# Gate logits of three of four chunks moved from TensorE to DVE, gate rows loaded earlier, key masks shared between DVE and POOL

## Chip, cores, metric

One core of a Trainium2 chip. The metric is device time in microseconds (us); lower is better. PE is TensorE, ACT is ScalarE, POOL is GpSimd, SP the queue that issues most DMAs, and PEld the weight loads, which run beside PE's matmuls.

## The reference, cut to what matters

A gate per token mixes an attention block with memory (four segments of 512 tokens, which the kernel calls chunks) and a gated feed-forward block.

```python
g = sigmoid((x * gate_w).sum(-1, keepdims=True))      # one logit per token: 2048 x 512 times 512
a = attention_with_memory(x, wq, wk, wv, wo, beta)     # 32 heads of 16, segments of 512, memory carried over
b = (relu(x @ W_gate) * (x @ W_up)) @ W_down           # 512 -> 1792 -> 512
return g * a + (1 - g) * b
```

## The kernel before: what the argument touches

The program describes every operation with its possible engines, an estimated duration, and the names that it reads and writes. A list scheduler in Python then walks through modelled time, puts each operation on an engine, and writes down one fixed instruction list per engine with semaphore waits. So any change of a duration or of an operation changes the order on all engines. Engines run their lists in order: a wait at the head of a list holds up everything behind it.

The loads, in order of issue (most on SP, two `wq` tiles on ACT):

```python
# hT0..3 (rows of x, chunk 0), wq, wk, wv, then:
load("sp", ["braw"], V.braw[:], A_beta.partition_broadcast(128), 8192)
load_gu(0)                                             # first halves of W_gate and W_up, 8 x 224 KB
load("sp", ["g4"], V.g4[:], gate_w.rearrange("(kt p) -> kt p", p=128), 1 << 12)   # the gate rows, 1 KB
load_gu(1)                                             # second halves
load_x(1)                                              # chunk 1 of x, 4 DMA transposes -> xT
load("sp", ["wo"], ...)
load("sp", ["wd"], V.wd[:], ..., NF * 128 * 1024)      # 1.8 MB, in one DMA
```

The gate logits: one small matmul turns the gate rows into columns (`gwT`), then one-column matmuls on PE, 16 for chunk 0 and 48 for chunks 1 to 3.

```python
gw_pe = pe(... matmul(A(ep_w)[:, 0:KT], lhsT=V.g4, rhs=V.ident[0:KT, 0:KT]) ..., name="gwT")
for part, (t0, t1) in enumerate(((0, 4), (4, NT))):
    def f_gmm(e, ...):
        for t in range(t0, t1):
            for kt in range(KT):
                ins = e.matmul(A(ep_g)[:, t - t0:t - t0 + 1], lhsT=V.xT[:, kt, t*128:(t+1)*128], rhs=V.gwc[:, kt:kt+1], ...)
```

Keys: `kT` is evicted, masked twice by DVE for the attention (`kmask`), and, for the memory, its exp goes into `ek`, is adjusted by DVE and transposed by a DMA into `phik`. `ek` has one buffer per head group, so the exp of the next chunk must wait until that transpose has read it.

```python
for p in range(2):
    evs.append(dve(... tensor_scalar(V.kp[:, ks, :], V.kT[:, G, :], V.pm[:, p:p+1], None, ALU.mult), 417, ...))   # kmask
acts.append(act(... activation(V.ek[:, G, :], V.kT[:, G, :], ACT.Exp) ..., writes=[f"ek{G}"]))
sps.append(dma("sp", ... dma_start_transpose(V.phik[:, :, G*128:(G+1)*128], V.ek[:, G, :]), reads=[f"ek{G}"], ...))
```

The softmax here doesn't subtract the row's maximum and nothing guards it: scores larger than these inputs give would overflow.

## Time and profile before

| | before |
|---|---|
| time, median of 6 runs | 276.43 us (275.97 to 276.89) |
| span of the profiled run | 274.8 us |
| first matmul, last matmul start | 1.25 us, 271.53 us |
| PE hole ahead of `gwT` | 0.82 us |
| 48 gate matmuls of chunks 1 to 3 | 1.2 us |

The busy line of the page of before, then the first two lines of its chain of waits (shares of the span, by engine and by line):

```profile
PE 269.2 (98%) x2205; PEld 116.2 (42%) x2205; DVE 200.1 (73%) x391; ACT 191.2 (70%) x167; POOL 91.4 (33%) x152
...
PE 91%; SPq 3%; DVE 2%; DMA 2%; issue 0%; ACT 0%
PE psA L731 37%; PE psA L770 18%; PE psL L661 9%; PE psA L686 7%; PE psA L566 7%; PE psA L564 5%; PE psA L763 5%; SPq L413 3%; DMA g<-in_gate_w_dram 2%; PE psA L607 1%; PE psA L636 1%; PE psA L522 1%; DVE ttmp L585 1%; DVE ek L586 0%; DVE rdm L629 0%
```

The chain is PE, but for one DMA: the 1 KB of gate rows. Here is that place in the timeline of PE (start, duration, engine, line, operation, count, idle time just before and what ended it):

```profile
13.72 0.40 PE L661 MATMUL psL<-qT,kp 32*128 32x512 bf16 x4
14.04 1.04 PE L564 MATMUL psA<-wv,xT 128*128 128x512 bf16 x4
15.73 0.17 PE L512 MATMUL psA<-ident,g 4*128 4x4 bf16 x1 [0.65 <-DMA g<-in_gate_w_dram]
```

Matmuls of 512 columns start every 0.216 us, and the printed ends are modelled. Four of them from 14.04 us are done streaming at 14.90 us, so PE stands still for 0.82 us, though the page prints 0.65. The gate matmuls of chunks 1 to 3:

```profile
54.59 1.34 PE L522 MATMUL psA<-gwc,xT 128*128 128x1 bf16 x48
55.87 0.40 PE L661 MATMUL psL<-qT,kp 32*128 32x384 bf16 x8
```

They take 25 ns each: 48 times 25 ns is 1.2 us for almost no arithmetic. The Trainium skill, "TensorE: Matmul & The Clock Gate", section "Wait — 56ns, not 53.3ns?", states this floor of about 25 ns between the starts of tiny matmuls, and the trace agrees (25.1 ns between the 48 starts). A third place that matters later are small holes where PE waits for DVE:

```profile
83.90 1.03 PE L566 MATMUL psA<-xT,wq 128*128 128x512 bf16 x4
84.98 1.04 PE L566 MATMUL psA<-xT,wk 128*128 128x512 bf16 x4
85.95 0.40 PE L661 MATMUL psL<-qT,kp 32*128 32x384 bf16 x8
86.51 2.33 PE L564 MATMUL psA<-wv,xT 128*128 128x512 bf16 x10 [0.17 <-DVE kT L579]
```

From 83.90 us four matmuls should end at 84.77; the next starts 0.21 us later. At 85.95 stand attention quads (a quad is four score matmuls of 32 rows that start within 0.01 us); the next matmul usually comes 0.33 us on; here 0.56. With one of 0.11 us at 117 us these holes make 0.55 us.

### The profile page before, as it was taken

The page shows a single profiled execution, that of the slowest core. Times are in us where ns is not written, and L with a number is a line of the kernel's source. Part 1 is how long each engine was busy: PE and PEld are TensorE (multiplying, and loading weights), DVE is VectorE, ACT ScalarE, POOL GpSimd, SP SyncE. Part 2 cuts the span into 40 slices and gives each one's busy share as a digit, 9 for nine tenths or more (in the row PEclk, how much of TensorE's full clock was granted, in tenths as well). Part 3 has the DMA queues.
Part 4 walks back from the last instruction along what each step waited for, and adds up shares of the span by engine and source line. Part 5 has one row for each costly group of instructions (what it writes and reads, how often), then busy time and mean ns, then how long its engine had stood idle before and what let it go on. Part 6 is the DMA issues. An engine that isn't in the chain of part 4 may idle for free.

```text
span 274.8 us, 5394 instructions
## 1 busy us (share of the span) xinstructions
PE 269.2 (98%) x2205; PEld 116.2 (42%) x2205; DVE 200.1 (73%) x391; ACT 191.2 (70%) x167; POOL 91.4 (33%) x152
## 2 busy tenths in 40 slices
PE   7999999999999999999999999999999999999995
PEld 3433434444343544534434444434444343444444
DVE  5779989999989969999789855396874256787200
ACT  3279898887787687778579777875867768773012
POOL 4013244353234434534243333243233343330000
PEclk9999999999999999999999999999999999999999
DMA  6999752100011122020012000100011100000011
GB/s 228 288 360 259 189 93 61 21 2 20 2 20 38 41 60 57 21 57 2 0 38 41 1 21 22 38 0 2 20 38 21 38 21 19 2 1 2 0 38 38
DMA packets 29152, 15.30 MB, mean 56 GB/s; under 512 B 20552, under 2 KB 29128, under 8 KB 29128
## 3 DMA queue, kind: packets, MB, share of 16 engines
q1 hardware_dynamic: 28552, 14.43, 20.6%
q10 hardware_dynamic: 576, 0.52, 0.6%
q8 instruction: 17, 0.28, 0.4%
q14 instruction: 7, 0.06, 0.1%
HBM read 8.14 MB, written 2.10 MB: 37 GB/s over the span
## 4 chain that ended last, share of the span: by engine, by line
PE 91%; SPq 3%; DVE 2%; DMA 2%; issue 0%; ACT 0%
PE psA L731 37%; PE psA L770 18%; PE psL L661 9%; PE psA L686 7%; PE psA L566 7%; PE psA L564 5%; PE psA L763 5%; SPq L413 3%; DMA g<-in_gate_w_dram 2%; PE psA L607 1%; PE psA L636 1%; PE psA L522 1%; DVE ttmp L585 1%; DVE ek L586 0%; DVE rdm L629 0%
## 5 line engine op out<-in xcount | busy, mean ns | idle before, releaser
L666 ACT ACTIVATE E<-psL 128x2048 bf16<-128x2048 f32 x80 | 150.1, 1876 | 41.3 <-PE psL L661 40.9
L669 POOL TENSOR_SCALAR_AFFINE_SELECT E<-E 128x512 bf16<-128x512 bf16 x128 | 81.3, 653 | 149.1 <-ACT E L666 134.0
L731 PE MATMUL psA<-xT,wu 128*128 128x512 bf16 x224 | 59.9, 380 | 0.0
L731 PE MATMUL psA<-xT,wg 128*128 128x512 bf16 x224 | 59.7, 380 | 0.0
L770 PE MATMUL psA<-wd,hT 128*128 128x512 bf16 (+1 forms) x238 | 54.3, 367 | 0.0
L742 DVE TENSOR_TENSOR hT<-psA,rl 128x512 bf16<-128x512 f32 x56 | 38.3, 684 | 12.6 <-PE psA L731 11.3
L661 PE MATMUL psL<-qT,kp 32*128 32x384 bf16 (+3 forms) x512 | 31.7, 301 | 0.0
L770 PEld LDWEIGHTS psA<-wd,hT 128*128 128x128 bf16 x238 | 21.8, 98 | 23.2 <-issue 3.0
L731 PEld LDWEIGHTS psA<-xT,wu 128*128 128x128 bf16 x224 | 20.6, 98 | 25.6 <-issue 2.0
L691 DVE STREAM_TRANSPOSE Tn<-psA 128x512 f32<-128x512 f32 x32 | 21.5, 700 | 13.0 <-PE psA L686 12.9
L731 PEld LDWEIGHTS psA<-xT,wg 128*128 128x128 bf16 x224 | 19.6, 98 | 24.6 <-issue 5.0
L739 ACT ACTIVATE rl<-psA 128x512 bf16<-128x512 f32 x30 | 17.8, 596 | 14.1 <-PE psA L731 14.1
L661 PEld LDWEIGHTS psL<-qT,kp 32*128 32x128 bf16 x512 | 8.9, 92 | 31.9 <-ACT E L666 14.4
L686 PE MATMUL psA<-E,vaug 128*17 128x256 bf16 (+3 forms) x512 | 21.0, 300 | 0.0
L740 DVE TENSOR_SCALAR rl<-psA 128x512 bf16<-128x512 f32 x26 | 17.8, 684 | 3.2 <-PE psA L731 2.5
L566 PE MATMUL psA<-xT,wq 128*128 128x512 bf16 x64 | 16.1, 380 | 0.3 <-DMA wq<-in_A_wq_dram 0.2
L763 PE MATMUL psA<-wo,oT 128*128 128x512 bf16 (+1 forms) x68 | 16.4, 367 | 0.0
L566 PE MATMUL psA<-xT,wk 128*128 128x512 bf16 x64 | 16.3, 380 | 0.1
L780 ACT ACTIVATE osb<-psA,omg 128x512 bf16<-128x512 f32 (+1 forms) x10 | 6.4, 644 | 14.1 <-PE psA L763 13.3
L564 PE MATMUL psA<-wv,xT 128*128 128x512 bf16 x64 | 15.5, 380 | 0.2 <-DVE kT L579 0.2
L686 PEld LDWEIGHTS psA<-E,vaug 128*17 128x17 bf16 x512 | 10.5, 90 | 11.0 <-issue 2.1
L779 DVE TENSOR_SCALAR osb<-psA,omg 128x512 bf16<-128x512 f32 x7 | 5.2, 745 | 12.6 <-PE psA L770 12.6
(71 smaller groups left out, 218.3 us busy)
## 6 DMA issues: line engine op xcount, KB each, us to landing
out_dram<-osb SPq DMA_DIRECT2D x15, 128.0 KB, 1.7
wg<-in_B_W_gate_dram SPq DMA_DIRECT2D x8, 224.0 KB, 4.9
wu<-in_B_W_up_dram SPq DMA_DIRECT2D x8, 224.0 KB, 5.5
wd<-in_B_W_down_dram SPq DMA_DIRECT2D x1, 1792.0 KB, 9.6
wk<-in_A_wk_dram SPq DMA_DIRECT2D x4, 128.0 KB, 4.4
wv<-in_A_wv_dram SPq DMA_DIRECT2D x4, 128.0 KB, 3.9
wo<-in_A_wo_dram SPq DMA_DIRECT2D x1, 512.0 KB, 5.1
hT<-in_A_x_dram SPq DMA_DIRECT2D x2, 128.0 KB, 2.7
```

The source lines that it names most:

```text
L564: ins = e.matmul(A(ep)[:, :], lhsT=V.xT[:, kt, tok + col * 128:tok + (col + 1) * 128], rhs=w[:, kt, :], start=(kt == 0), stop=(kt == KT - 1))
L566: ins = e.matmul(A(ep)[:, :], lhsT=w[:, kt, col * 128:(col + 1) * 128], rhs=V.xT[:, kt, tok:tok + 512], start=(kt == 0), stop=(kt == KT - 1))
L661: ins = q.matmul(PL[:, jj, o:o + w], lhsT=V.kp[32 * jj:32 * jj + 32, kslot(s, n), 128 * j:128 * j + 128], rhs=V.qT[32 * jj:32 * jj + 32, q ...
L666: acts.append(act(lambda a, e=e: a.activation(V.E[:, e, :, :], PL[:, :, :], ACT.Exp, scale=SCALE), t_act(2048), reads=[f"bankL{b}" for b i ...
L669: pools.append(pool(lambda g, ap=ap: g.affine_select(out=ap, in_=ap, compare_op=ALU.is_ge, fill=0.0, base=0, pattern=[[0, 4], [1, 128]], c ...
L686: ins = q.matmul(A(ep)[32 * jj:32 * jj + 17, c:512], lhsT=V.vaug[:, s % 2, j, 8 * G + 2 * jj + p, :], rhs=V.E[:, e, jj, o:o + w], start=(j ...
L691: ds.append(dve(lambda e, p=p, ep=eps[p]: e.transpose(V.Tn[:, p, :], A(ep)[:, :]), t_dve(512), writes=[f"Tn{p}"], name=f"tr{s}_{G}_{p}", e ...
L731: ins = e.matmul(A(ep)[:, :], lhsT=w[:, kt, f * 128:(f + 1) * 128], rhs=V.xT[:, kt, c * 512:(c + 1) * 512], start=(kt == 0), stop=(kt == K ...
L739: evs.append(sc.add(Op([("act", lambda e, ep=eg, r=r: e.activation(V.rl[:, r, :], A(ep)[:, :], ACT.Relu), t_act(512)), ("dve", lambda e, e ...
L742: evs.append(dve(lambda e, ep=eu, r=r, hs=hs: e.tensor_tensor(V.hT[:, hs, :], A(ep)[:, :], V.rl[:, r, :], ALU.mult), t_dve(512), reads=[f" ...
L763: ins = e.matmul(A(ep)[:, 0:c1 - c0], lhsT=V.oT[:, o0 + G, i * 128:(i + 1) * 128], rhs=V.wo[:, G, c0:c1], start=st_ and G == 0, stop=sp_ a ...
L770: ins = e.matmul(A(ep)[:, 0:c1 - c0], lhsT=V.hT[:, slots[f], i * 128:(i + 1) * 128], rhs=V.wd[:, f, c0:c1], start=st_ and f == f0, stop=sp ...
```

## The change

Its intent is to shorten PE's list (DVE computes 12 of the 16 tiles' logits), to end the wait for the gate rows, and to relieve DVE of key masks where POOL is free. Cut to its core:

```diff
 # loads
+    load("act", ["g4"], V.g4[:], gate_w..., 1 << 12)          # right behind wq on the ACT queue
     load_gu(0)
-    load("sp", ["g4"], V.g4[:], gate_w..., 1 << 12)
     load_gu(1)
     load_x(1)
+    load("sp", ["gwb"], V.gwb[:], gate_w.partition_broadcast(128), 1 << 17)
 # gate logits: chunk 0 on PE as before; chunks 1 to 3:
+            for t in range(t0, t1):
+                ld = dma("sp", ... dma_start(V.osb[:, 2, :], A_x[0, t*128:(t+1)*128, :]) ..., name=f"ldxr{t}")
+                ld.after = GATE_T[c] + 4000.0 * (t - t0)      # 44, 90, 140 us
+                gq["dve"].append(dve(... tensor_tensor_reduce(out=V.osb[:, 2, :], in0=V.osb[:, 2, :], in1=V.gwb[:], op0=ALU.mult, op1=ALU.add, accum_out=V.gl[:, t:t+1]) ...))
+            gq["act"].append(act(... activation(gx, V.gl[:, t0:t1], ACT.Exp) ...))
 # ... omg, gexpT copies and c2g per chunk instead of in two parts (64 small copies instead of 32)
 # key masks of chunks 1 to 3
-                evs.append(dve(... tensor_scalar(V.kp..., V.kT..., V.pm[:, p:p+1], None, ALU.mult), 417, ...))
+                alts = [("dve", km, 390)] + ([("pool", km, 680)] if s else [])
+                evs.append(sc.add(Op(alts, ...)))
 # output staging of chunks 0 to 2 uses two buffers of three; modelled time of the denominator matmuls halved
```

The full diff also reads `gexpT`, `c2g` and `omg` by chunk; nothing else depends on it.

More of the change, by code (lines that the diff above doesn't have):

```diff
@@ L16 @@
 SWITCH = 100.0
+GATE_T = {1: 44000.0, 2: 90000.0, 3: 140000.0}
 def mm(n, k=1):
@@ L353, in plan @@
         ("gwc", [128, KT], BF16), ("braw", [128, 32], BF16), ("eb", [128, 32], F32), ("romgh", [128, 32], F32), ("epsv", [128, 32], F32),
-        ("gexp", [128, NT], F32), ("omg", [128, NT], F32), ("gexpT", [128, NT * 4], F32), ("c2g", [128, NT, 32], F32),
+        ("gexp", [128, NT], F32), ("omg", [128, NT], F32), ("gexpT", [128, NT * 4], F32), ("c2g", [128, 2, 4, 32], F32), ("gwb", [128, 512], BF16), ("gl", [128, NT], F32),
         ("rden", [128, 32], F32), ("rdg", [128, 32], F32), ("rdm", [128, 128], F32), ("pm8", [128, 8], F32), ("pm", [128, 2], F32), ("ident", [128, 128], BF16), ("g4", [4, 128], BF16),
@@ L419, in program @@
             load("act" if nm == "wq" and kt % 2 else "sp", [f"{nm}{kt}"], w[:, kt, :], src[kt * 128:(kt + 1) * 128, :], 1 << 17)
+    load("act", ["g4"], V.g4[:], gate_w.rearrange("(kt p) -> kt p", p=128), 1 << 12)
     half = (NF // 2) * 128
@@ L434, in program @@
     load_gu(0)
-    load("sp", ["g4"], V.g4[:], gate_w.rearrange("(kt p) -> kt p", p=128), 1 << 12)
     load_gu(1)
     load_x(1)
+    load("sp", ["gwb"], V.gwb[:], gate_w.partition_broadcast(128), 1 << 17)
     load("sp", ["wo"], V.wo[:], A_wo.rearrange("(g p) n -> p g n", p=128), 1 << 19)
@@ L514, in program @@
     gexpT_r = {}
-    gq = {"pe": [], "act": [], "dve": [], "flex": []}
-    for part, (t0, t1) in enumerate(((0, 4), (4, NT))):
-        ep_g = Epoch()
-        def f_gmm(e, t0=t0, t1=t1, ep_g=ep_g):
-            for t in range(t0, t1):
-                for kt in range(KT):
-                    ins = e.matmul(A(ep_g)[:, t - t0:t - t0 + 1], lhsT=V.xT[:, kt, t * 128:(t + 1) * 128], rhs=V.gwc[:, kt:kt + 1], start=(kt == 0), stop=(kt == KT - 1))
-            return ins
-        gq["pe"].append(pe(f_gmm, (t1 - t0) * KT * 26.0, reads=[x for c in range(t0 // 4, t1 // 4) for x in xt(c)] + ["gwc"], name=f"gmm{part}", ep=ep_g, role="w"))
-        gx = V.gexp[:, t0:t1]
-        gq["act"].append(act(lambda e, t0=t0, t1=t1, gx=gx, ep_g=ep_g: e.activation(gx, A(ep_g)[:, 0:t1 - t0], ACT.Exp), 190, writes=[f"gexp{part}"], name="gexp", ep=ep_g, role="r"))
+    gq = {"pe": [], "act": [], "dve": [], "flex": [], "sp": []}
@@ new lines, in program, with f_gmm @@
+    for c in range(NSEG):
+        t0, t1 = 4 * c, 4 * c + 4
+        gx = V.gexp[:, t0:t1]
+        if c == 0:
+            ep_g = Epoch()
+            def f_gmm(e):
+                for t in range(4):
+                    for kt in range(KT):
+                        ins = e.matmul(A(ep_g)[:, t:t + 1], lhsT=V.xT[:, kt, t * 128:(t + 1) * 128], rhs=V.gwc[:, kt:kt + 1], start=(kt == 0), stop=(kt == KT - 1))
+                return ins
+            gq["pe"].append(pe(f_gmm, 4 * KT * 26.0, reads=xt(0) + ["gwc"], name="gmm", ep=ep_g, role="w"))
+            gq["act"].append(act(lambda e, gx=gx: e.activation(gx, A(ep_g)[:, 0:4], ACT.Exp), 190, writes=[f"gexp{c}"], name="gexp", ep=ep_g, role="r"))
+        else:
+            for t in range(t0, t1):
+                ld = dma("sp", lambda e, t=t: e.dma_start(V.osb[:, 2, :], A_x[0, t * 128:(t + 1) * 128, :]), 1 << 17, writes=["osb2_0", "osb2_1"], name=f"ldxr{t}")
+                ld.after = GATE_T[c] + 4000.0 * (t - t0)
+                gq["sp"].append(ld)
+                gq["dve"].append(dve(lambda e, t=t: e.tensor_tensor_reduce(out=V.osb[:, 2, :], in0=V.osb[:, 2, :], in1=V.gwb[:], scale=1.0, scalar=0.0, op0=ALU.mult, op1=ALU.add, accum_out=V.gl[:, t:t + 1]),
+                                     t_dve(512) + 70, reads=["osb2_0", "osb2_1", "gwb"], writes=["osb2_0", "osb2_1", f"gl{t}"], name=f"gate{t}"))
+            gq["act"].append(act(lambda e, t0=t0, t1=t1, gx=gx: e.activation(gx, V.gl[:, t0:t1], ACT.Exp), 215, reads=[f"gl{t}" for t in range(t0, t1)], writes=[f"gexp{c}"], name="gexp"))
@@ L527, in program @@
         om = V.omg[:, t0:t1]
-        gq["dve"].append(dve(lambda e, om=om, gx=gx: e.tensor_scalar(om, gx, 1.0, None, ALU.add), 180, reads=[f"gexp{part}"], writes=[f"omg1{part}"], name="omg1"))
-        gq["dve"].append(dve(lambda e, om=om: e.reciprocal(om, om), 250, reads=[f"omg1{part}"], writes=[f"omg{part}"], name="omg"))
-        gexpT_r[part] = []
+        gq["dve"].append(dve(lambda e, om=om, gx=gx: e.tensor_scalar(om, gx, 1.0, None, ALU.add), 180, reads=[f"gexp{c}"], writes=[f"omg1{c}"], name="omg1"))
@@ L531, in program @@
+        gq["dve"].append(dve(lambda e, om=om: e.reciprocal(om, om), 250, reads=[f"omg1{c}"], writes=[f"omg{c}"], name="omg"))
+        gexpT_r[c] = []
         for a in range(4):
@@ L535, in program, with c2g @@
                                              ("act", lambda e, a=a, dst=dst, t0=t0, t1=t1: e.activation(dst, V.gexp[32 * a:32 * a + 32, t0:t1], ACT.Copy), 215)],
-                                            reads=[f"gexp{part}"], writes=[f"gexpT{part}_{a}{jj}"], name="gexpT")))
-                gexpT_r[part].append(f"gexpT{part}_{a}{jj}")
-        if part:
-            gq["dve"].append(dve(lambda e, t0=t0: e.tensor_tensor(V.c2g[:, t0:, :], V.eb[:, :].unsqueeze(1).to_broadcast([128, NT - t0, 32]), V.gexp[:, t0:].unsqueeze(2).to_broadcast([128, NT - t0, 32]), ALU.mult),
-                                 t_dve((NT - t0) * 32), reads=["eb", f"gexp{part}"], writes=["c2g"], name="c2g"))
-    sc.queue(2, [gw_pe] + gq["pe"][:1])
-    sc.queue(4, gq["pe"][1:])
+                                            reads=[f"gexp{c}"], writes=[f"gexpT{c}_{a}{jj}"], name="gexpT")))
+                gexpT_r[c].append(f"gexpT{c}_{a}{jj}")
+    def c2g(s):
+        t0 = 4 * s
+        return dve(lambda e: e.tensor_tensor(V.c2g[:, s % 2, :, :], V.eb[:, :].unsqueeze(1).to_broadcast([128, 4, 32]), V.gexp[:, t0:t0 + 4].unsqueeze(2).to_broadcast([128, 4, 32]), ALU.mult),
+                   t_dve(128), reads=["eb", f"gexp{s}"], writes=[f"c2g{s % 2}"], name=f"c2g{s}")
+    sc.queue(2, [gw_pe] + gq["pe"])
     sc.queue(1, [gw_act] + gq["act"])
@@ L545, in program @@
     sc.queue(2, gq["flex"])
+    sc.queue(3, gq["sp"])
     def kslot(s, n):
@@ L581, in proj @@
                 ks = kslot(s, 2 * G + p)
-                evs.append(dve(lambda e, G=G, p=p, ks=ks: e.tensor_scalar(V.kp[:, ks, :], V.kT[:, G, :], V.pm[:, p:p + 1], None, ALU.mult), 417, reads=[f"kT{G}", "pm"], writes=[f"kp{ks}"], name=f"kmask{s}_{G}_{p}"))
+                km = lambda e, G=G, p=p, ks=ks: e.tensor_scalar(V.kp[:, ks, :], V.kT[:, G, :], V.pm[:, p:p + 1], None, ALU.mult)
+                alts = [("dve", km, 390)] + ([("pool", km, 680)] if s else [])
+                evs.append(sc.add(Op(alts, reads=[f"kT{G}", "pm"], writes=[f"kp{ks}"], name=f"kmask{s}_{G}_{p}")))
             if s < NSEG - 1:
@@ L616, in nd @@
     def nd(s):
-        pes, ds, sps = [], [], []
+        pes, ds, sps = [], [c2g(s)], []
         ep = Epoch()
@@ L625, in fden @@
             return ins
-        pes.append(pe(fden, 16 * 60, reads=[f"phiq{G}" for G in range(4)] + ["Mbd16"], name=f"den{s}", ep=ep, role="w"))
+        pes.append(pe(fden, 16 * 30, reads=[f"phiq{G}" for G in range(4)] + ["Mbd16"], name=f"den{s}", ep=ep, role="w"))
         ds.append(dve(lambda e: e.tensor_tensor(V.rdm[:, :].rearrange("q (i h) -> q i h", i=4), A(ep)[:, 0:128].rearrange("q (i h) -> q i h", i=4),
@@ L629, in nd @@
         ds.append(dve(lambda e: e.reciprocal(V.rdm[:], V.rdm[:]), 920, reads=["rdm"], writes=["rdm"], name=f"ndr{s}"))
-        ds.append(dve(lambda e: e.tensor_tensor(V.rdm[:, :], V.rdm[:, :], V.c2g[:, 4 * s:4 * s + 4, :].rearrange("q i h -> q (i h)"), ALU.mult), t_dve(128), reads=["rdm", "c2g"], writes=["rdm"], name=f"ndc{s}"))
+        ds.append(dve(lambda e: e.tensor_tensor(V.rdm[:, :], V.rdm[:, :], V.c2g[:, s % 2, :, :].rearrange("q i h -> q (i h)"), ALU.mult), t_dve(128), reads=["rdm", f"c2g{s % 2}"], writes=["rdm"], name=f"ndc{s}"))
         for i in range(4):
@@ L695, in flush @@
             ds.append(dve(lambda e: e.reciprocal(rv, Tv[:, :, :, 16]), 345, reads=["Tn0", "Tn1"], writes=["rden"], name=f"rden{s}_{G}"))
-            ds.append(dve(lambda e: e.tensor_tensor(gv, rv, V.gexpT[:, 16 * s:16 * s + 16].unsqueeze(1).to_broadcast([128, 2, 16]), ALU.mult), 264, reads=["rden"] + gexpT_r[min(s, 1)], writes=["rdg"], name=f"rdg{s}_{G}"))
+            ds.append(dve(lambda e: e.tensor_tensor(gv, rv, V.gexpT[:, 16 * s:16 * s + 16].unsqueeze(1).to_broadcast([128, 2, 16]), ALU.mult), 264, reads=["rden"] + gexpT_r[s], writes=["rdg"], name=f"rdg{s}_{G}"))
             av = V.adT[:, :].rearrange("q (c p e) -> q p c e", p=2, e=16)
@@ L775, in outp @@
                 tiles.append(pes)
-                r = t % 3
+                r = t % 3 if last else t % 2
                 om = V.omg[:, t:t + 1]
@@ L780, in outp @@
                                       ("act", lambda e, ep=ep, r=r, om=om, c0=c0, c1=c1: e.activation(V.osb[:, r, c0:c1], A(ep)[:, 0:c1 - c0], ACT.Copy, scale=om), t_act(w, True, 1))],
-                                     reads=[f"omg{min(s, 1)}"], writes=res, name=f"fin{s}_{i}", ep=ep, role="r")))
+                                     reads=[f"omg{s}"], writes=res, name=f"fin{s}_{i}", ep=ep, role="r")))
                 sps.append(dma("sp", lambda e, r=r, t=t, c0=c0, c1=c1: e.dma_start(out[0, t * 128:(t + 1) * 128, c0:c1], V.osb[:, r, c0:c1]), w * 256,
```

## The prediction

> **What bounds the kernel now.** TensorE. The page gives PE 98% busy (269.2 of 274.8 us), DVE 73%, ACT 70%, POOL 33%; the chain that ended last is 91% PE. In the timeline matmuls follow each other every 0.2165 us (512 columns) without holes; each attention quad costs 0.33 us plus about 0.09 us ahead of it. From 20 to 250 us the windows view shows PE busy 229.8 of 230 us, so time saved on another engine is worth nothing there. Only fewer PE instructions, holes in PE, and the two ends can shorten the span. First matmul (1.25 us) and tail (only PE work from about 249 us) are not touched. DVE is the second limit: 36.9 of 40, 44.8 of 50 and 44.4 of 50 us between 20 and 160 us.
>
> **What the change takes away.**
> - 48 gate matmuls of one column (chunks 1 to 3): 1.18 us of PE, 54.76 to 55.94 us, on the chain.
> - The wait for the gate rows. They are issued 17th on the SP queue, at 10.90 us, and are on the chain for 4.79 us; PE stands still from about 14.91 to 15.73 us: 0.8 us. Issued on the ACT queue after wq (about 2.7 us) they land by about 7 us. The extra issue (0.47 us) pushes ACT's table load, but ACT then idles 0.68 us before its first xT copy, so that copy should not move.
> Together 2.0 us on the critical path.
>
> **What it adds, none of it on PE.**
> - 12 row loads of 128 KB on SP (0.45 us issue each; the same size landed in 2.7 us).
> - 12 multiply-and-sums on DVE; none is in the trace. Estimate from the 128x512 tensor_tensor forms (0.41 to 0.69 us): 0.7 to 0.9 us, 10 us in all.
> - gexpT copies: 64 instead of 32 (0.17 to 0.26 us each), 7 us shared by DVE and ACT; omg and c2g about 1 us.
> - Key masks of chunks 1 to 3, 24 at 0.34 to 0.40 us on DVE, may go to POOL: up to 9 us off DVE. On POOL I expect 0.5 to 0.8 us each (its 128x512 selects take 0.65). The Trainium skill, "SBUF — State Buffer", section "Who interferes with whom", says that DVE and GpSimd share a port pair under an exclusive lock; the trace fits so far as masks on DVE range from 0.31 to 0.85 us.
> So DVE stays within 6 us of 200, ACT +4, POOL +8.
>
> **How much is on the path.** The 2.0 us. But every engine's order is computed anew by the program's list scheduler, with other durations (the denominator matmuls at half; 16 take 0.41 us). The number of tile-mode switches stays; how many stand side by side (saving 0.1 us each) may differ by a few: +-0.5 us. Output staging of chunks 0 to 2 drops from three buffers to two and SP waits in order, so a row load behind a store, or DVE waiting for a row, can make a new hole: I allow 0 to 1 us.
>
> **Prediction.** 274.6 us, range 273.2 to 276.4. Faster by over 2%: 0.03; within 2%: 0.95; slower by over 2%: 0.02.
>
> **What shows it right.** No PE hole at 15 us, gate rows not in the chain; 16 instead of 64 gate matmuls; PE still 97 to 98% busy and over 90% of the chain; DVE 195 to 206 us busy; the multiply-and-sum at 0.7 to 0.9 us; no PE wait released by a row load.
>
> **What would make it wrong.** Slower: DVE held by late rows or by POOL's masks between 40 and 110 us, so evictions come late and PE waits; transposes late behind row loads on SP; the first xT copy delayed. Faster: a reordering that removes many mode switches, or more holes than I see.

## The result

The changed kernel takes 275.31 us (median of 6 runs, 275.20 to 275.55) against 276.43 us (6 runs). A ratio in this text is the mean time of one kernel's fast runs over the mean of the other's of the same rounds, so it is not quite the ratio of the medians. Here it is 0.9961, 95% interval 0.9947 to 0.9974: 1.1 us less, where 2.0 had been forecast. The result is inside the forecast range, but about half of one of the two stated savings is missing and a loss was added. Lying inside proves little: the stated range, 273.2 to 276.4 us, reaches up to the time of before, and the misses partly cancel. The lines that answer to those of before, first the page:

```profile
PE 263.7 (96%) x2122; PEld 115.8 (42%) x2157; DVE 206.3 (75%) x402; ACT 198.4 (73%) x205; POOL 120.6 (44%) x167
...
PE 90%; DMA 4%; issue 2%; ACT 1%; DVE 1%; ACTq 1%
PE psA L747 35%; PE psA L786 18%; PE psL L677 9%; PE psA L580 8%; PE psA L702 7%; PE psA L578 5%; PE psA L779 5%; DMA phik<-ek 3%; DMA g<-in_gate_w_dram 2%; PE psA L652 1%; PE psA L623 1%; ACT E L682 1%; ACTq L414 1%; PE psA L639 0%; DVE ek L602 0%
```

PE's 96% is no loss of density: 2157 weight loads stand beside 2122 matmuls, so 35 matmul records are missing, each worth 0.216 us of "idle". The chain is the better witness, and it names two DMAs: the gate rows are still there, and a transpose `phik<-ek` is new. The gate rows and PE, at the start:

```profile
6.93 0.17 PE L514 MATMUL psA<-ident,g 4*128 4x4 bf16 x1
7.14 1.09 PE L580 MATMUL psA<-xT,wq 128*128 128x512 bf16 x4
8.07 0.54 PE L527 MATMUL psA<-gwc,xT 128*128 128x1 bf16 x16
```

The hole at 15 us is gone and only 16 gate matmuls are left. But the scheduler now puts `gwT` ahead of the first q projection. The weight-load row of the timeline shows what it waited for:

```profile
6.93 0.09 PEld L514 LDWEIGHTS psA<-ident,g 4*128 4x128 bf16 x1 [0.60 <-DMA g<-in_gate_w_dram]
```

The new hole is at 35 us. ACT first, then PE:

```profile
31.11 0.62 ACT L589 ACTIVATE phiq<-qT 128x512 bf16<-128x512 bf16 x1
33.57 0.63 ACT L600 ACTIVATE ek<-kT 128x512 bf16<-128x512 bf16 x1 [1.84 <-DMA phik<-ek]
34.11 1.86 ACT L682 ACTIVATE E<-psL 128x2048 bf16<-128x2048 f32 x1
```

```profile
34.55 0.59 PE L747 MATMUL psA<-xT,wg 128*128 128x512 bf16 x2
36.02 0.40 PE L677 MATMUL psL<-qT,kp 32*128 32x256 bf16 x8 [0.87 <-ACT E L682]
```

ACT waits 1.84 us for a transpose of chunk 0's keys to leave `ek`; its next attention exp is late, PE's next quad waits for that exp. Counted by starts of matmuls PE loses 0.94 us here and 0.19 us just before, at 34.07 us. The stretch of the chain that leads there, and the issue order of the SP queue:

```profile
26.60 6.95 DMA phik<-ek
33.55 0.02 issue
33.57 0.63 ACT ek L600
34.20 1.77 ACT E L682
```

```profile
22.35 0.51 SPq L414 DMA_DIRECT2D wd<-in_B_W_down_dram  x1
26.60 5.19 SPq L603 DMA_TRANSPOSE phik<-ek  x3
```

A transpose that usually lands 2.4 us after issue took 6.95 us, with the 1.8 MB load of `wd` ahead of it on the same queue.

The small holes of before at 84, 86 and 117 us are not in the changed kernel. The two new kinds of work, by the query for a line (durations in ns, minimum, median, maximum):

```profile
L536 DVE CUSTOM_DVE_ANT_0 osb<-osb,gwb x12: 650/689/1116, 54.2 to 163.7; 128x512 bf16<-128x512 bf16 x12
L536 DVE DVE_READ_ACCUMULATOR2_ANT gl<- x12: 74/80/84, 55.2 to 164.3; 128x1 f32 x12
...
L596 DVE TENSOR_SCALAR kp<-kT,pm x17: 336/353/791, 14.2 to 154.6; 128x512 bf16<-128x512 bf16 x17
L596 POOL TENSOR_SCALAR kp<-kT,pm x15: 1559/1564/1989, 27.3 to 160.0; 128x512 bf16<-128x512 bf16 x15
```

The multiply-and-sum is as cheap as estimated. It shows as two instructions; the Trainium skill, "VectorE: DVE Perf Modes", section "Two Vector instructions with no wait between them", says that an operation that also writes out its accumulator is two, and the trace agrees (0.69 and 0.08 us). A key mask on POOL takes 1.56 us, 4.4 times its time on DVE and 2.3 times what the scheduler was told.

### Where 1.35 us of span went

The spans of the two profiled runs differ by 1.35 us (274.80 and 273.45). From the starts of PE's instructions, less 0.216 us per 512 columns, with missing records filled in from the weight loads:

| part | us |
|---|---|
| chunk 1's first q projection starts at 24.04 instead of 24.46 | -0.42 |
| 48 gate matmuls less | -1.20 |
| new holes at 34 and 35 us | +1.13 |
| holes at 84, 86 and 117 us gone | -0.55 |
| last matmul to end of span, 3.06 instead of 3.27 | -0.21 |
| rest | -0.10 |

### The profile page after: what moved, and what is told of

It is laid out like the page before. It is cut to its first block, busy times and chain, and to the rows that moved or that the text cites. A ratio compares the mean times of both kernels' runs of the same rounds, so it can differ in the third digit from the quotient of the medians.

```text
span 273.4 us, 5333 instructions
## 1 busy us (share of the span) xinstructions
PE 263.7 (96%) x2122; PEld 115.8 (42%) x2157; DVE 206.3 (75%) x402; ACT 198.4 (73%) x205; POOL 120.6 (44%) x167
## 4 chain that ended last, share of the span: by engine, by line
PE 90%; DMA 4%; issue 2%; ACT 1%; DVE 1%; ACTq 1%
PE psA L747 35%; PE psA L786 18%; PE psL L677 9%; PE psA L580 8%; PE psA L702 7%; PE psA L578 5%; PE psA L779 5%; DMA phik<-ek 3%; DMA g<-in_gate_w_dram 2%; PE psA L652 1%; PE psA L623 1%; ACT E L682 1%; ACTq L414 1%; PE psA L639 0%; DVE ek L602 0%
## 5 line engine op out<-in xcount | busy, mean ns | idle before, releaser
L685 POOL TENSOR_SCALAR_AFFINE_SELECT E<-E 128x512 bf16<-128x512 bf16 x128 | 86.1, 690 | 125.2 <-ACT E L682 125.1
L747 PE MATMUL psA<-xT,wg 128*128 128x512 bf16 x213 | 57.2, 380 | 1.7 <-issue 1.7
L747 PE MATMUL psA<-xT,wu 128*128 128x512 bf16 x218 | 58.0, 380 | 0.7 <-issue 0.5
L786 PE MATMUL psA<-wd,hT 128*128 128x512 bf16 (+1 forms) x230 | 53.5, 367 | 0.9 <-issue 0.6
L596 POOL TENSOR_SCALAR kp<-kT,pm 128x512 bf16<-128x512 bf16 x15 | 24.6, 1640 | 1.3 <-DVE kT L593 1.0
L755 ACT ACTIVATE rl<-psA 128x512 bf16<-128x512 f32 x27 | 16.1, 596 | 11.9 <-PE psA L747 11.0
L756 DVE TENSOR_SCALAR rl<-psA 128x512 bf16<-128x512 f32 x29 | 19.8, 684 | 5.4 <-PE psA L747 4.5
L796 ACT ACTIVATE osb<-psA,omg 128x512 bf16<-128x512 f32 (+1 forms) x12 | 7.8, 651 | 15.3 <-PE psA L779 13.3
L580 PE MATMUL psA<-xT,wk 128*128 128x512 bf16 x62 | 15.5, 379 | 0.2 <-issue 0.2
```

The source lines that it names most:

```text
L580: ins = e.matmul(A(ep)[:, :], lhsT=w[:, kt, col * 128:(col + 1) * 128], rhs=V.xT[:, kt, tok:tok + 512], start=(kt == 0), stop=(kt == KT - 1))
L596: km = lambda e, G=G, p=p, ks=ks: e.tensor_scalar(V.kp[:, ks, :], V.kT[:, G, :], V.pm[:, p:p + 1], None, ALU.mult)
L685: pools.append(pool(lambda g, ap=ap: g.affine_select(out=ap, in_=ap, compare_op=ALU.is_ge, fill=0.0, base=0, pattern=[[0, 4], [1, 128]], c ...
L747: ins = e.matmul(A(ep)[:, :], lhsT=w[:, kt, f * 128:(f + 1) * 128], rhs=V.xT[:, kt, c * 512:(c + 1) * 512], start=(kt == 0), stop=(kt == K ...
L786: ins = e.matmul(A(ep)[:, 0:c1 - c0], lhsT=V.hT[:, slots[f], i * 128:(i + 1) * 128], rhs=V.wd[:, f, c0:c1], start=st_ and f == f0, stop=sp ...
```

## The experiments

My theory: the gate matmuls are worth their 1.2 us; the early gate rows are worth less than 0.8 us, as something else bounds the start; and the `wd` load, through the transposes, takes back over 1 us. The rivals: the terms were mis-sized from the start, since DVE and ACT give the time back (then removing PE work alone buys little); or the hole comes of the slow masks on POOL.

Kernels named b_ are the kernel before with an edit, a_ the changed kernel with an edit. Unless it says "new orders", the edit is made after scheduling, so that the compute engines keep the order of their lists. Each was timed in 5 rounds beside the kernel before, whose median was 276.64 to 276.69 us.

### b_g4_early: the gate rows alone

```diff
-  SP:  ... wu0 x4, g4, wg1 x4 ...
+  ACT: hT, hT, wq, wq, g4        (own semaphore)
```

> Kernel before with one thing changed: the gate rows are issued on the ACT queue behind wq; the order of every other instruction is kept. My accounting: the PE hole of 0.81 us before the small gate-row matmul goes, so 0.6 to 0.9 us less than before (ratio 0.9968 to 0.998), no hole above 0.2 us between 14 and 16 us. Rival (PE is late for other reasons and the next wait eats the gain): within 0.2 us of before.

Measured: 276.29 us, ratio 0.9987 (0.9975 to 0.9999): 0.36 us, half of the forecast. In its trace the hole ahead of `gwT` is 0.10 us, and one of 0.12 us is new ahead of chunk 1's first q projection. Chunk 1's x, which that projection needs, landed at 24.08 us, and its first weight load started 0.21 us later, the same step as in b_both below. So the wait can be ended, but its 0.8 us are not all gained.

### b_one_gate: the gate matmuls alone

```diff
-            for t in range(4, 16): for kt in range(4): matmul(ps[:, t], xT..., gwc[:, kt])     # 48
+            matmul(ps[:, 0:12], lhsT=xT[:, 0, 512:640], rhs=ident[:, 0:12])                   # 1, wrong on purpose
```

> Kernel before with the 48 one-column gate matmuls of chunks 1 to 3 replaced by one matmul of 12 columns (gate values wrong on purpose), all orders kept. My accounting: 47 x 25 ns = 1.17 us less (1.0 to 1.3 us; ratio about 0.9958). Rival (evictions on DVE and the exps on ACT set the pace there and give it back): under 0.5 us.

Measured: 275.52 us, ratio 0.9959 (0.9947 to 0.9971): 1.13 us, close to the 1.18 us that 47 times 25 ns come to. Its output is wrong, which doesn't matter for the time. This term of the prediction is right, and the rival that DVE and ACT would give it back falls.

### b_both: both edits

> Both edits at once, wrong gate values on purpose. If the two terms of the prediction are right and add up: 2.0 us less than before (1.7 to 2.2; ratio about 0.993), which is 0.9 us better than the change itself, so the change loses 0.9 us elsewhere. If the sum itself was mis-sized: about 1.1 us, as the change shows.

Measured: 275.44 us, ratio 0.9958 (0.9946 to 0.9970): 1.16 us. The two savings do not add up: the early gate rows bought nothing here. The weight-load row of PE's timeline shows why it can't:

```profile
23.05 0.11 PEld L733 LDWEIGHTS psA<-xT,wg 128*128 128x128 bf16 x2 [0.23 <-issue]
24.64 0.56 PEld L568 LDWEIGHTS psA<-xT,wq 128*128 128x128 bf16 x4 [1.49 <-issue]
```

PE stood still for 1.19 us ahead of chunk 1's first q projection (two matmuls from 23.05 us are done streaming at 23.48, the next starts at 24.67; the printed 1.49 is idle time of the weight loads, not of PE). That projection needs the transposed x of chunk 1. The last of its four loads landed at 24.43 us in this trace, 0.21 us before the weight load. The chain of waits names a small DVE copy that ended at 24.59 us, because it was the last event before the start; the instruction waits on five semaphores, and that copy is a coincidence, as the next run shows.

### b_both_x1: the same, with chunk 1's x loaded sooner

```diff
-  SP: ... wg1 x4, wu1 x4, ldx1 x4 (transposes), wo, wd ...
+  SP: ... ldx1 x4 (transposes), wg1 x4, wu1 x4, wo, wd ...
```

> b_both (gate rows early, one small gate matmul for chunks 1 to 3, wrong gate values on purpose) with the four transposed loads of chunk 1's x issued ahead of the second halves of the gate and up weights; compute orders kept. b_both won 1.16 us, not 2.0, and its trace has a PE hole of 1.2 us at 23.3 us, ahead of chunk 1's first q projection, with those loads landing at 24.43. If that landing ate the gain of the early gate rows: loads land before 21 us, hole gone, 0.7 to 1.2 us less than b_both, about 2.0 us less than before (ratio 0.992 to 0.9935). If the gain was lost elsewhere: ratio stays at 0.9958.

Measured: 274.96 us, ratio 0.9935 (0.9921 to 0.9949): 1.8 us less than before, and in medians 0.5 us less than b_both. It was run at another time. The loads land by 21.88 us, the projection starts at 23.29 us with no hole, while the DVE copy of b_both still ends after 24.2 us. So the landing of chunk 1's x was the second bound, right behind the gate rows:

```profile
22.84 0.11 PEld L733 LDWEIGHTS psA<-xT,wg 128*128 128x128 bf16 x2 [0.23 <-issue]
23.08 0.74 PEld L568 LDWEIGHTS psA<-xT,wq 128*128 128x128 bf16 x4
```

The remainder to 2.0 us shows too: a hole of 0.31 us at 40.4 us, where ACT's key exp waited 1.1 us for `phik<-ek`. It is the changed kernel's hole, in the order of before, and this edit made it: SP issued the reordered loads later, `wd` at 24.90 us (b_both: 22.07), and the first transpose, issued at 27.97, took 10.01 us to land.

### a_wd_late: the big load behind the transposes

```diff
-  SP: ... wo, wd, phik x3, ldx ...
+  SP: ... wo, phik x3, wd, ldx ...
```

> The changed kernel with one thing moved: the 1.8 MB load of the down weights is issued behind the third transpose of chunk 0's keys instead of ahead of it; every other order and every wait kept. If that load holds up the transposes (first one 6.95 us to landing), and through ACT's key exp makes the PE hole of 0.94 us at 34.8 us and the one of 0.19 us before it: first transpose under 4 us to landing, hole gone, 0.9 to 1.1 us less than the change, about 2.1 us less than before (ratio 0.992 to 0.993). Rival (the hole comes from slow key masks on POOL or from DVE): hole stays, time as the change, ratio 0.996.

Measured: 274.06 us, ratio 0.9910 (0.9895 to 0.9924): 2.5 us less than before, 1.25 us less than the change by the medians, and correct. The span of the profiled run went from 273.4 to 272.3 us. Its SP queue, and ACT and PE in place of the lines shown of the change:

```profile
26.66 4.46 SPq L603 DMA_TRANSPOSE phik<-ek  x3
31.17 0.57 SPq L414 DMA_DIRECT2D wd<-in_B_W_down_dram  x1
```

```profile
31.10 0.62 ACT L589 ACTIVATE phiq<-qT 128x512 bf16<-128x512 bf16 x1
31.62 0.62 ACT L600 ACTIVATE ek<-kT 128x512 bf16<-128x512 bf16 x1
32.14 1.87 ACT L682 ACTIVATE E<-psL 128x2048 bf16<-128x2048 f32 x1
```

```profile
34.35 0.59 PE L747 MATMUL psA<-xT,wg 128*128 128x512 bf16 x2
34.87 0.40 PE L677 MATMUL psL<-qT,kp 32*128 32x256 bf16 x8
```

The transposes land 2.4 us after issue, ACT does not wait, the quad comes 1.15 us sooner (34.87 for 36.02). Nothing was gained before it: chunk 1's first q projection starts at 24.03 us, in the change at 24.04. The key masks on POOL still take 1.56 us each, so the rival cause of this hole falls. The Trainium skill, "DMA: Bandwidth & Descriptors", section "Queues, rings and completion order", says that on each DMA engine the descriptors of a queue are consumed in ring order. The traces agree: the three transposes behind `wd` landed after 6.95, 5.44 and 4.10 us, ahead of it after 2.46, 2.41 and 2.42 us. Whether `wd` on another queue would have held them up as well was not tried.

### b_wd_late: nearly the same move, behind the first transpose, in the order of before

```diff
-  SP: ... wo, wd, phik, ldx x4 ...
+  SP: ... wo, phik, wd, ldx x4 ...
```

> Kernel before with the down-weights load issued behind the first transpose of chunk 0's keys; compute orders kept. My theory says that the load only hurts the order of the changed kernel, which asks for the first key exp of chunk 1 at 31.7 us (before: 37.96 us): so before should not move, ratio 0.998 to 1.002. Rival (the moved load is good in itself, by less DMA traffic at the start): ratio under 0.996, as in a_wd_late.

Measured: 276.73 us, ratio 0.9999 (0.9981 to 1.0016): nothing. The load stood ahead of the transpose in the kernel before too (issued at 21.77 and 29.14 us), but there the transpose landed at 32.38 us and ACT asks for `ek` only at 37.96 us. So the loss belongs to the new order, not to the load as such.

### a_mask_dve_wd and a_mask_cost_wd: is the sharing of masks worth its price?

```diff
 # a_mask_dve_wd (new orders, wd late)
-                alts = [("dve", km, 390)] + ([("pool", km, 680)] if s else [])
+                alts = [("dve", km, 390)]
 # a_mask_cost_wd (new orders, wd late)
+                alts = [("dve", km, 390)] + ([("pool", km, 1570)] if s else [])
```

> The changed kernel, down-weights load late as in a_wd_late, key masks on DVE alone (the scheduler computes new orders). If the POOL sharing pays, by relieving DVE where before had three PE holes of 0.55 us in all between 83 and 117 us: such holes come back, 0.3 to 1.0 us slower than a_wd_late (ratio 0.992 to 0.995 of before). If the sharing is worthless or harmful, as a mask takes 1.56 us on POOL against 0.35 us on DVE: equal to or faster than a_wd_late (ratio 0.991 or less).

Measured: 274.63 us, ratio 0.9920 (0.9905 to 0.9935). Of the DVE holes two small ones are there, 0.08 us at 51 and 0.16 us at 118 us; those at 84 and 86 us did not return.

> The changed kernel, down-weights load late, with POOL's key mask entered into the scheduler at the measured 1570 ns instead of 680 ns (new orders). If the mis-sized cost makes worse orders: fewer masks on POOL and up to 0.5 us faster than a_wd_late (ratio 0.989 to 0.991). If POOL has slack enough that it does not matter: within 0.3 us of a_wd_late (0.990 to 0.992).

Measured: 274.74 us, ratio 0.9927 (0.9910 to 0.9945). The scheduler still puts 11 masks on POOL (15 before). Telling it the true cost did not help; small holes of 0.11 to 0.35 us stand between 72 and 81 us. This run also shows the start at its worst:

```profile
2.67 4.97 DMA g<-in_gate_w_dram
7.64 0.05 issue
7.69 0.17 PE psA L514
7.86 0.04 issue
7.90 1.02 PE psA L580 x4
```

The gate rows landed at 7.64 us and the first q projection started at 7.90.

### a_wd_late2 and a_mask_dve_wd2: both again, on one chip

> a_wd_late again, as the reference for the other three of this call: ratio 0.990 to 0.992 of before, no PE hole over 0.2 us after 8 us; the gate-row matmul just before the first q projection waits for the gate rows, which land at 6.9 to 7.7 us.

Measured: 274.27 us, ratio 0.9912 (0.9898 to 0.9927). The trace of this run has all 2157 matmul records, PE is 98% busy, and no hole above 0.1 us is left after 8 us.

> a_mask_dve_wd again, beside a_wd_late2 on one chip: if the sharing of key masks with POOL pays, 0.3 us or more slower than a_wd_late2; if it is worth nothing, within 0.3 us.

Measured: 274.58 us (274.31 to 275.14), ratio 0.9926 (0.9912 to 0.9939). Without POOL's help it is 0.3 us slower, the second time in the same direction; the intervals overlap and the orders differ, so the sharing is worth 0.3 us at most and is not shown to be worth anything.

### a_wd_gf: the gate rows ahead of wq

```diff
-  ACT: hT, hT, wq, wq, g4
+  ACT: hT, hT, g4, wq, wq
```

> a_wd_late with the gate rows issued on the ACT queue ahead of its two wq loads instead of behind them; every other order kept. The change moved the wait for the gate rows from 15 us to about 7 us, as its schedule puts the gate-row matmul ahead of the first q projection, which started at 7.14 to 7.90 us in four traces of the changed kernel and at 6.08 to 7.17 us in six of the kernel before. If the rows still hold up the start: first q projection at 6.1 to 7.1 us, 0.2 to 0.6 us less than a_wd_late2, unless chunk 1's x (lands at 23.4 us, needed at 24.0) takes it back. If the start is late for the clock or wq alone: within 0.1 us of a_wd_late2.

Measured: 274.08 us (273.72 to 274.26), ratio 0.9904 (0.9889 to 0.9918): 0.2 us less than a_wd_late2 by the medians, inside the scatter. In the trace the first q projection starts at 6.64 us, 0.46 us sooner, and the third matmul of it then waits for `wq` itself. Inconclusive in time.

### a_wd_gf_x1: and chunk 1's x ahead

> a_wd_gf with chunk 1's transposed x loads ahead of the second halves of the gate and up weights too. If both bounds of the start are real: 0.4 to 0.9 us less than a_wd_late2, ratio 0.988 to 0.990 of before, the fastest of all. Rival (weights then come late and make a hole at 35 to 41 us, as the 0.31 us one in b_both_x1): equal to a_wd_gf or slower.

Measured: 273.74 us (273.51 to 273.89), ratio 0.9892 (0.9878 to 0.9906), correct, the fastest of all, and 0.5 us below a_wd_late2, whose runs took 273.91 to 274.50 us. Its single trace does not show that gain: span 272.1 against 272.2 us, chunk 1's q projection at 23.88 against 23.91 us. So where the half microsecond comes from stays open, and the intervals touch.

### The start, over all traces

| | first q projection | chunk 1's first q projection |
|---|---|---|
| kernel before and its edits, six traces | 6.08 to 7.17, mean 6.51 | 24.46, 25.17, 24.50 where the gate rows come late |
| changed kernel and its edits with g4 behind wq, six traces | 7.10 to 7.90, mean 7.33 | 23.91 to 24.71, mean 24.16 |

So the change starts its first projection 0.8 us later than before, and is ahead by only 0.55 us at chunk 1 (24.71, the mean of the three, less 24.16). Part of the spread is the PE clock: in the trace of before the last transpose of chunk 0's x started at 4.85 us, in others as late as 5.39, with the same instructions, because the 128-column matmuls there start 0.107 us apart for longer before going over to 0.056. The Trainium skill, "TensorE: Matmul & The Clock Gate", section "What's actually happening", puts this down to an activity window that runs freely; the traces agree in that the step comes at different times in different runs. In before, the wait for the gate rows at 15 us absorbs such a late start; in the changed kernel it is passed on. So the hole ahead of `gwT` is not a fixed 0.8 us either: it is 1.50 us in b_wd_late, whose third q matmul starts 0.63 us sooner than in before, and 1.22 us in b_one_gate, where the rows land at 16.39 us.

What holds the start of the changed kernel differs from trace to trace. In a_wd_late2, a_mask_dve_wd and a_mask_cost_wd it is the gate rows alone: they landed at 6.84, 7.20 and 7.64 us, and `gwT` started 0.05 us later. In a_wd_late and a_mask_dve_wd2 the rows were there 0.18 and 0.70 us before `gwT`, which stood behind the last of the ten warm-up matmuls (`psL<-rl`, on a constant tile), in these traces 0.38 to 0.43 us apart to the end. In the trace of the change itself two waits coincide: the rows landed at 6.89 us and the last part of `wq` at 7.51. The third matmul of the projection, the first to need that part, started at 7.64 us; for the gate rows alone it could have started at about 7.58, two matmuls after the first. In before it started at 7.14, with `wq` in at 7.09. So 0.51 us were lost there, and earlier gate rows alone would not have won them back in that trace. This accounts for the table's 0.42 us: 0.82 of the hole and 0.11 of `gwT`, which no longer stands behind that matmul, less 0.51.

## Why the prediction was right or wrong

1. **PE bounds the kernel; time saved elsewhere is worth nothing.** Right in its first half: b_one_gate took 1.18 us of matmuls off PE's list and the time fell by 1.13 us, with the work of DVE and ACT unchanged. The second half was not tested by itself, and a_wd_late limits it: moving one DMA bought 1.25 us, by closing a PE hole that the new order had opened.
2. **48 gate matmuls, 1.18 us.** Right, by the same run.
3. **The wait for the gate rows, 0.8 us.** This is the term that was mis-sized. The hole was real, but "Together 2.0 us on the critical path" took for granted that nothing came right behind it. Two things did, one in each order. The changed schedule asks for the rows at 6.9 us, about when they land, so the wait moved to the start, where the load of `wq` and the warm-up matmuls end at nearly the same time; the prediction gave the landing time correctly ("about 7 us") but never asked when the new order would need them. In the order of before, chunk 1's x lands at 23.7 to 24.4 us, just when PE gets there with the gate rows early; in the change it landed at 23.27, 0.77 us ahead of need, and was no bound. In the order of before the term was worth 0.36 us (0.03 to 0.69, b_g4_early), and nothing that shows beside the gate matmuls (b_both); in the changed kernel's trace 0.42 us. With chunk 1's x moved ahead the pair comes to 1.8 us (b_both_x1).
4. **New holes, 0 to 1 us allowed.** They came to 1.13 us in the trace, and moving one load buys 1.25 us. The kind was near what I named ("transposes late behind row loads on SP"), the culprit was not: no row load, but the `wd` load that was there all the time, and an ACT exp that the new order asks for 6 us sooner. a_wd_late and b_wd_late together show this.
5. **What I did not foresee on the good side.** Three holes of 0.55 us in all, where PE waited for DVE, are not in the new order. I had read PE as free of holes, since the page counts only idle time between modelled ends. Whether masks on POOL or the new order as such removed them is not settled: without POOL two small ones stood elsewhere.
6. **Costs off the path.** The multiply-and-sum was right (0.80 us mean, and 0.08 for the accumulator). Masks on POOL were not: 1.56 us, not 0.5 to 0.8; POOL's sum rose by 29 us, not 8. ACT rose by 7 us, not 4, since 53 of the 64 small copies went there. DVE came to 206.3 us, just over the stated 195 to 206. Of these only the masks were tested, and taking them off POOL made nothing faster; what the rest costs was not measured.
7. **The signs named in advance.** Right: no hole at 15 us, 16 gate matmuls, PE about 90% of the chain, no PE wait ended by a row load; PE's 96% on the page is short of the stated 97 to 98% by the missing records. Wrong: the gate rows are still in the chain, at 2%.

The stated 274.6 us was 0.7 us too low. In sum: about 0.4 us of the gate rows' 0.8 was missing and 1.13 us of new holes came instead of the 0 that the point assumed, against 0.55 us of old holes gone and 0.2 us at the end.

## What to carry to other kernels

A wait that stands in the chain is worth at most the distance to the next wait behind it: before counting it as gained, look up when the next operands land and when the new order will ask for the same one. In a kernel whose order is computed from estimated durations, removing work moves everything else, and an early bulk load that had hurt nobody may then stand ahead of a small transfer that is now urgent; keep big loads that are needed late behind small ones that are needed soon. Change one order at a time after scheduling: that separates the gain of an edit from the luck of the order.

## What the Trainium skill lacked or had wrong

- "GPSIMD Engine Reference", section "4.1 Engine selection", calls one-input elementwise work on GpSimd "roughly line-rate". A 128x512 bf16 multiply by a per-partition scalar took 1.56 us on POOL and 0.35 us on DVE; the select of the same size on POOL took 0.65 to 0.69 us on average. No page has a time for this multiply.
- "DMA: Bandwidth & Descriptors", section "Rules for kernel authors", advises to issue a DMA early and to wait late. It lacks the price: with a 1.8 MB load issued 4 us ahead of it on the same queue, a transpose took 6.95 us to land instead of 2.46, and issuing that load 9 us later made the kernel 1.25 us faster.
- No page says that a trace can lack matmul records at fixed places: here 35 or 36 of 2157 to 2205 in nine of fourteen profiles, none in the other five, which shows as 2 points less of PE busy time.
